# Constants first on GpSimd, and attention steps dealt out anew over the feed-forward phases

## The chip, the cores and the metric

The kernel runs on one core of one Trainium2 chip. The metric is the device time of one execution in microseconds, as the median of several runs. The core's engines are TensorE (PE, with its weight loads shown as PEld), VectorE (DVE), ScalarE (ACT), GpSimd (POOL) and SyncE (SP, used here only to issue transfers). PE matmuls write to PSUM, which has eight banks; everything else lives in SBUF or in device memory.

## The reference, cut to what matters

Everything is float32. First comes attention with a memory, for 4 batches, 8 heads, 576 positions and head width 64:

```python
scores = scale * q @ k.T                       # causal mask, softmax
local = softmax(scores) @ v
q_p = phi(q)                                   # elu(q) + 1
mem_out = (q_p @ M_prev) / (q_p @ z_prev + 1e-6)
g = sigmoid(beta)                              # one per head
attn = g * mem_out + (1 - g) * local
x = attn as 2304 tokens x 512
x = softplus(x @ w1_in) @ w1_out               # 512 -> 2048 -> 512
y = elu(x @ w2_in) @ w2_out                    # 512 -> 2048 -> 512
```

## The kernel before, in words

**Tiling of the feed-forward work.** The 2304 tokens are cut into five chunks (`CHUNKS`) of 512, 512, 448, 416 and 416 columns. A phase is one chunk through one layer, `ffn(c, layer)`. Its first half goes over 16 tiles of the inner width: each has 12 matmuls (4 slices of the contraction, three products of split values: high by high, high by low, low by high, lines 573 to 575), an activation on ACT and DVE (`act`, lines 547 to 560), and a split of the result into a high and a low part (lines 577 and 578). Its second half has 16 weight tiles with 12 matmuls each (lines 589 to 591). So there are ten phases of 384 matmuls, 32 weight tiles each, in the order that the list `order` in `TUNE` gives: chunks 0 and 1 through layer 1, the same two through layer 2, and then chunks 2, 3 and 4, both layers each.

**Weights.** They come as 64-bit numbers and are converted once each: a load on SP's queue (L504), one operation on ACT (L507) and two on DVE (L508, L509) that make a 32-bit float, a rounding copy on ACT (called through L97), a subtraction on DVE (L516), and a store of both parts to scratch memory on SP's queue (L518). Later uses load from scratch (`s_0i`, `s_0o`, `s_1i`, `s_1o`, L533). `weights` fetches a tile from scratch if it is there and converts it in place if not. The preamble converts 14 tiles of `w1_in` among its attention steps; the other weights of layer 1 are converted where phase 1 uses them. `conversions()` is a generator that converts weights of layer 2 ahead of use, into scratch, one tile per step.

**Attention** is a generator too, `attention(b, part, ...)`. Part A of a batch is its first 256 positions (21 steps), part B its last 320 (43 steps). A step issues scores on PE, the mask, scale and row minimum in one DVE instruction (L319), the exponential on ACT (L325), normalisation, transposes on PE against the identity (L360, L260), the products with v and with the memory (L375, L377, L385), and the transfers for later heads on POOL's queue (L172, L173, L180, L191 to L210). `chain` strings batches together. The preamble runs part A of batches 0 and 1; `sides()` then runs part A of batches 2 and 3 and part B of all four.

**What sets the order.** At the end of the file a loop walks the phases. Each entry of `order` holds, for either half of a phase, two shares per weight tile: how many attention steps and how many conversions are put out there. They are summed up, and a step is put out whenever the sum passes one. Attention steps are put out with a priority 400 ahead of their place, weight loads 200 ahead. The framework's planner then fixes each engine's instruction order by these priorities and by a simulation of its own; on the chip each engine works its list in that order.

**The start.** `early_loads` issues the transfers of batch 0 on SP's queue. `constants()` is called after it: the load of `beta` on POOL's queue (L110), the identity (a memset and a select on POOL, in the helper masks.py, called at L111), the mask (a memset on DVE, L112, and a select on POOL, L113), ones, and from `beta` the two gates `ig` and `iomg` on ACT and DVE (L118 to L122). A memset on POOL of a tile that only a loop of zero length (`still`) would read stands at L647, and `pads()` (L132) clears the ends of the score buffers.

Of the kernel before, what the change touches and what calls it, by code (L numbers as in the profile page):

```python
# [8 lines left out]
F32 = mybir.dt.float32  # L9
# [9 lines left out]
KD = DM // 128  # L19
# [16 lines left out]
WIDTH = [sum(n for _, _, n in c) for c in CHUNKS]  # L36
SLOT = (0, 1, 2, 0, 1)
TUNE = dict(
    st='q', pri=(200, 200), conv=(4, 2, 14), inw=4, still=0, ahead=(3, 3, 0), plain=(0, 1, 2, 3),
    hi='ssss ssss', lo='v', sc='vv vvv ssv', pt='s ssv', eva='sv',  # L40


    order=((0, 0, (1.9, 0.0), (1.1, 0.0)), (1, 0, (0.4, 0.2), (0.9, 0.9)), (0, 1, (0.9, 0.0), (0.9, 0.0)), (1, 1, (1.0, 0.0), (1.3, 0.0)), (2, 0, (0.4, 0.0), (1.2, 0.0)), (2, 1, (0.8, 0.0), (1.2, 0.0)), (3, 0, (0.4, 0.0), (1.2, 0.0)), (3, 1, (0.8, 0.0), (1.0, 0.0)), (4, 0, (0.0, 0.0), (0.0, 0.0)), (4, 1, (0.0, 0.0), (0.0, 0.0))),
)


# [12 lines left out]
def kernel(  # L59
# [14 lines left out]
    nc = tc.nc  # L74
    ve, se, ge, te = nc.vector, nc.scalar, nc.gpsimd, nc.tensor
# [9 lines left out]
    psf = ctx.enter_context(tc.tile_pool(name="psf", bufs=4, space=bass.MemoryType.PSUM))  # L85
# [4 lines left out]
    T = TUNE  # L90

    def f32(ap):
        return ap.bitcast(F32)
# [8 lines left out]
    bsb = const.tile([128, H], F32, name="bsb")  # L102
    ident = const.tile([128, 128], F32, name="ident")
    mask = const.tile([128, QP], F32, name="mask")
# [2 lines left out]
    iomg = const.tile([128, H], F32, name="iomg")  # L107

    def constants():
        nc.gpsimd.dma_start(bsb, beta)  # L110
        make_identity(nc, ident)  # L111
        ve.memset(mask, 0.0)  # L112
        ge.affine_select(  # L113
            out=mask[:, 512:640], in_=mask[:, 512:640], pattern=[[-1, 128]],
            compare_op=ALU.is_ge, fill=NEG, base=0, channel_multiplier=1,
        )
        ve.memset(ones, 1.0)
        se.activation(ig, bsb, ACTF.Exp, scale=-1.0)  # L118
        ve.tensor_scalar(ig, ig, 1.0, None, ALU.add)
        ve.reciprocal(iomg, ig)  # L120
        ve.tensor_scalar(iomg, iomg, -1.0, 1.0, ALU.mult, ALU.add)
        ve.reciprocal(iomg, iomg)  # L122

    sph = [const.tile([128, SOFF[4] + QP], F32, name=f"sph{i}") for i in range(2)]
    slots = [[const.tile([128, 2, 512], F32R, name=f"x{c}_{k}") for k in range(KD)] for c in range(2)]
# [4 lines left out]
    def pads():  # L130
        for t in sph:
            ge.memset(t[:, SOFF[4] + S:], 0.0)  # L132
# [397 lines left out]
    def make(src, key, pool=None):  # L530
        w = (pool or wp).tile([128, 2, 4, 128], F32R, name="w", tag="g" if pool else "w")
        if key in scratch:
            nc.sync.dma_start(f32(w), scratch[key])  # L533
        else:
            convert(src, key, w)
        return w
# [70 lines left out]
    def early_loads(pool):  # L607

        d = {key: [] for key in ("kq", "q", "z", "v", "m")}
        for p in range(NP):  # L610
            if p % 2 == 0:
                pair = gp.tile([128, 2, 512], F32, name="kq", tag="g")
            kq = pair[:, p % 2, :]
            t = pool.tile([128, 6, 128], F32, name=f"ar0_{p}")
            for h in range(2):
                own = slice(64 * h, 64 * h + 64)
                nc.sync.dma_start(kq[own], ak[p, own, h, :])
            nc.sync.dma_start(t, ar[p])
            d["kq"].append(kq)
            d["q"].append(t[:, 0:2, :])  # L620
            d["z"].append(t[:, 2:3, :])
            d["v"].append(t[:, 3:5, :].rearrange("p h (t c) -> p h t c", t=2))
            d["m"].append(t[:, 5, :].rearrange("p (h c) -> p h c", h=2))
        return d
# [3 lines left out]
    def chain(parts, ahead):  # L628

        parts, active = list(parts), []  # L630
        while parts or active:
            if parts and (not active or len(active) == 1 and active[0][2] <= ahead):
                b, part, pool, early = parts.pop(0)
                active.append([(b, part), attention(b, part, pool, early), 21 if part == "A" else 43])
            for a in list(active):
                a[2] -= 1
                if next(a[1], a) is a:
                    active.remove(a)
                    ready.add(a[0])
                else:  # L640
                    yield

    with tc.tile_pool(name="pre", bufs=1) as pre, tc.tile_pool(name="pre3", bufs=2) as pre3:
        loads = early_loads(pre)
        constants()
        still = slots[1][KD - 1]
        ge.memset(f32(still), 0.0)  # L647
        k = 0
        begin, step, count = T["conv"]
        for _ in chain(((0, "A", pre3, loads), (1, "A", pre3, None)), T["ahead"][0]):  # L650
            if k == 0:
                pads()
            if k >= begin and (k - begin) % step == 0 and len(made) < count:
                key = f"0i{len(made)}"
                made[key] = make(w1i[len(made)], key, gp if len(made) < count - T["inw"] else None)
            for _ in range(T["still"]):
                h = psf.tile([128, 512], F32, name="h", tag="h")
                tc.keep_in_program_order(te.matmul(h, still[:, 0, 0:128], still[:, 0, :], start=True, stop=True))
            k += 1
    late = ctx.enter_context(tc.tile_pool(name="late", bufs=1))  # L660
    slots.append([late.tile([128, 2, WIDTH[2]], F32R, name=f"x2_{k}") for k in range(KD)])
# [98 lines left out]
```

## Time and profile before

| what | value |
|---|---|
| median of 3 runs | 1108.59 us (1107.11 to 1111.91) |
| the profiled execution | 1105.83 us |
| its span, first to last instruction | 1104.1 us |
| PE busy | 1058.9 us, 96% of the span |
| PE weight loads busy | 913.4 us, 83% |
| DVE busy | 688.0 us, 62% |
| ACT busy | 672.2 us, 61% |
| POOL busy | 91.1 us, 8% |
| transfers | 252.71 MB, 229 GB/s on the mean |

The profile lists each instruction with its engine and its line in the program. Busy time is the union of the spans of an engine's instructions. The granted clock of PE is given as a share of full speed (2.4 GHz). The DMA share is the mean busy share of the core's 16 DMA engines. A name such as `w<-in_w2i` is the tile written and the tile or tensor read.

### The profile page before, as it was taken

Reading aid. Unit: us, or ns where it says so; the run is one execution under the profiler, and the core shown is the slowest. Engines: PE = TensorE matmul, PEld = TensorE weight load, DVE = VectorE, ACT = ScalarE, POOL = GpSimd, SP = SyncE. Lnnn points to the kernel's source line nnn. Section 1 sums busy time; section 2 is a strip of 40 time slices with the busy share of each in tenths; the row PEclk is TensorE's granted clock in tenths of the full one; section 3 lists DMA queues with packets and bytes.
Section 4 is the critical chain, followed back from the end, with each engine's and each line's share of the span. In section 5 each row is a group of like instructions: output and inputs, shape, how many; then the busy total and the mean of one; then the engine's idle time right before and its main releaser. Section 6 shows DMA issues by size and latency. Waiting matters only on the chain.

```text
span 1104.1 us, 15804 instructions
## 1 busy us (share of the span) xinstructions
PE 1058.9 (96%) x5328; PEld 913.4 (83%) x5328; DVE 688.0 (62%) x1698; ACT 672.2 (61%) x1458; POOL 91.1 (8%) x173
## 2 busy tenths in 40 slices
PE   4799999999899999999999999999999999999998
PEld 2356766767687888888889999999999999999998
DVE  5974686677776788688746755984576472150540
ACT  4755885478875896567747964664696452290330
POOL 6123132100000000100000000000000000000000
PEclk8778999999999999999999999999999999999999
DMA  9891278768899758955666656657755567877785
GB/s 283 302 297 50 84 242 265 244 223 279 295 314 340 256 197 303 328 192 182 197 205 222 227 176 231 218 186 234 241 174 182 172 212 237 258 235 232 227 236 179
DMA packets 73409, 252.71 MB, mean 229 GB/s; under 512 B 10352, under 2 KB 14960, under 8 KB 73328
## 3 DMA queue, kind: packets, MB, share of 16 engines
q1 hardware_dynamic: 64720, 217.61, 59.0%
q0 software_dynamic: 8608, 34.09, 10.2%
q8 instruction: 42, 0.69, 0.3%
q14 instruction: 39, 0.32, 0.1%
HBM read 213.39 MB, written 38.27 MB: 228 GB/s over the span
## 4 chain that ended last, share of the span: by engine, by line
PE 80%; DMA 9%; DVE 7%; ACT 2%; issue 1%; SPq 0%; POOL 0%; DVEq 0%; ACTq 0%
PE h L573 11%; PE h L574 11%; PE h L575 11%; PE h L589 10%; PE h L591 10%; PE h L590 10%; PE tp L360 4%; PE o L377 2%; PE o L385 2%; DMA s_1i<-w 2%; PE s L297 2%; DMA w<-in_w2i 2%; DMA w<-in_w2o 2%; PE o L375 2%; DMA w<-in_w1i 1%; PE s L293 1%
## 5 line engine op out<-in xcount | busy, mean ns | idle before, releaser
L573 PE MATMUL h<-x,w 128*128 128x512 f32 (+2 forms) x640 | 239.4, 379 | 8.4 <-DVE t L552 4.2
L589 PE MATMUL h<-g,w 128*128 128x512 f32 (+2 forms) x640 | 238.2, 374 | 2.6 <-DMA w<-s_0o 2.6
L574 PE MATMUL h<-x,w 128*128 128x512 f32 (+2 forms) x640 | 240.1, 375 | 0.0
L575 PE MATMUL h<-x,w 128*128 128x512 f32 (+2 forms) x640 | 239.2, 374 | 0.0
L591 PE MATMUL h<-g,w 128*128 128x512 f32 (+2 forms) x640 | 238.4, 373 | 0.0
L590 PE MATMUL h<-g,w 128*128 128x512 f32 (+2 forms) x640 | 238.4, 373 | 0.0
L573 PEld LDWEIGHTS h<-x,w 128*128 128x128 f32 x640 | 121.0, 190 | 25.7 <-DVE t L552 5.8
L589 PEld LDWEIGHTS h<-g,w 128*128 128x128 f32 x640 | 120.8, 189 | 15.2 <-DMA w<-s_0o 3.1
L574 PEld LDWEIGHTS h<-x,w 128*128 128x128 f32 x640 | 121.2, 189 | 13.3 <-issue 1.7
L575 PEld LDWEIGHTS h<-x,w 128*128 128x128 f32 x640 | 121.3, 190 | 12.8
L591 PEld LDWEIGHTS h<-g,w 128*128 128x128 f32 x640 | 120.7, 189 | 12.6 <-issue 1.4
L590 PEld LDWEIGHTS h<-g,w 128*128 128x128 f32 x640 | 120.9, 189 | 11.9 <-issue 0.7
L578 DVE TENSOR_TENSOR g<-t,g 128x512 fp32r<-128x512 f32 (+2 forms) x160 | 100.7, 633 | 31.3 <-ACT g L577 30.4
L325 ACT ACTIVATE sph<-sph,neg 128x576 f32<-128x576 f32 (+3 forms) x160 | 96.2, 602 | 35.4 <-DVE neg L319 34.9
L577 ACT CAST g<-t 128x512 fp32r<-128x512 f32 (+2 forms) x160 | 91.4, 574 | 31.0 <-DVE t L560 25.6
L552 DVE SCALAR_TENSOR_TENSOR t<-h,t 128x512 f32<-128x512 f32 (+2 forms) x80 | 50.4, 635 | 56.6 <-ACT t L551 56.2
L365 ACT CAST ptb<-tp 128x512 fp32r<-128x512 f32 (+2 forms) x96 | 44.2, 498 | 55.0 <-PE tp L360 54.7
L366 DVE TENSOR_TENSOR ptb<-tp,ptb 128x512 fp32r<-128x512 f32 (+2 forms) x96 | 53.0, 574 | 38.2 <-ACT ptb L365 37.6
L319 DVE CUSTOM_DVE_ANT_0 sph<-s,mask 128x128 f32<-128x128 f32 (+4 forms) x80 | 38.4, 482 | 60.1 <-PE s L297 39.9
L360 PE MATMUL tp<-ident,sph 128*128 128x128 f32 x480 | 71.1, 282 | 0.2 <-DVE sph L335 0.2
L507 ACT ACTIVATE wr<-w 128x512 f32<-128x512 f32 x64 | 42.8, 669 | 41.7 <-DMA w<-in_w2i 15.0
L360 PEld LDWEIGHTS tp<-ident,sph 128*128 128x128 f32 x480 | 59.8, 146 | 8.2 <-DVE sph L335 1.5
(112 smaller groups left out, 1539.2 us busy)
## 6 DMA issues: line engine op xcount, KB each, us to landing
w<-s_1i SPq DMA_DIRECT2D x80, 512.0 KB, 3.9
w<-s_1o SPq DMA_DIRECT2D x65, 512.0 KB, 4.2
w<-s_0i SPq DMA_DIRECT2D x64, 512.0 KB, 4.2
w<-s_0o SPq DMA_DIRECT2D x64, 512.0 KB, 4.3
qk<-in_qk POOLq DMA_DIRECT2D x32, 480.0 KB, 5.5
w<-in_w1i SPq DMA_DIRECT2D x16, 512.0 KB, 5.5
s_0i<-w SPq DMA_DIRECT2D x16, 512.0 KB, 4.4
w<-in_w1o SPq DMA_DIRECT2D x16, 512.0 KB, 4.7
```

The lines of the kernel that those rows point to most:

```text
L325: se.activation(Pi, Pi, ACTF.Exp, scale=-1.0, bias=neg[:, i:i + 1], accum_out=sums(n, i))
L360: te.transpose(pt[:, c:c + 128], P[:, poff(n, i) + 128 * j:poff(n, i) + 128 * j + 128], ident)
L366: ve.tensor_sub(dst[:, 1, :c], pt[:, :c], f32(dst)[:, 0, :c])
L552: ve.scalar_tensor_tensor(t, h, 0.0, t, ALU.max, ALU.add)
L573: te.matmul(h[:, :N], hi[:, k, :], xk[:, 0, :N], start=k == 0, stop=False)
L574: te.matmul(h[:, :N], hi[:, k, :], xk[:, 1, :N], start=False, stop=False)
L575: te.matmul(h[:, :N], lo[:, k, :], xk[:, 0, :N], start=False, stop=k == KD - 1)
L577: se.copy(g[:, 0, :N], t[:, :N])
L578: ve.tensor_sub(g[:, 1, :N], t[:, :N], f32(g)[:, 0, :N])
L589: te.matmul(h[:, :N], hi[:, k, :], gs[f][:, 0, :N], start=f == 0, stop=False)
L590: te.matmul(h[:, :N], hi[:, k, :], gs[f][:, 1, :N], start=False, stop=False)
L591: te.matmul(h[:, :N], lo[:, k, :], gs[f][:, 0, :N], start=False, stop=f == KF - 1)
```

## The change

`constants()` is called ahead of `early_loads` and with a priority of 1000. Inside it POOL now makes the part of the mask that holds the triangle by itself (memset and select), then the identity, and then issues the load of `beta`; DVE clears only the rest of the mask. The memset of L647 and the empty loop go. The place of `pads()` becomes an entry of `TUNE`, with the same value, zero. In `order` the shares of the first four phases are other numbers: fewer attention steps in the second half of phase 1 and in phase 2, more in phases 3 and 4; conversions ahead of layer 2 begin in the second half of phase 1 and are fewer in the second half of phase 2.

```diff
 TUNE = dict(
-    st='q', pri=(200, 200), conv=(4, 2, 14), inw=4, still=0, ahead=(3, 3, 0), plain=(0, 1, 2, 3),
+    st='q', pri=(200, 200), conv=(4, 2, 14), inw=4, ahead=(3, 3, 0), pads=0, plain=(0, 1, 2, 3),
...
-    order=((0, 0, (1.9, 0.0), (1.1, 0.0)), (1, 0, (0.4, 0.2), (0.9, 0.9)), (0, 1, (0.9, 0.0), (0.9, 0.0)), (1, 1, (1.0, 0.0), (1.3, 0.0)), (2, 0, ...
+    order=((0, 0, (1.9, 0.0), (0.8, 0.2)), (1, 0, (0.2, 0.2), (0.8, 0.6)), (0, 1, (1.1, 0.0), (1.2, 0.0)), (1, 1, (1.1, 0.0), (1.5, 0.0)), (2, 0, ...
 )
@@ constants()
-        nc.gpsimd.dma_start(bsb, beta)
-        make_identity(nc, ident)
-        ve.memset(mask, 0.0)
+        ge.memset(mask[:, 512:640], 0.0)
         ge.affine_select(
             out=mask[:, 512:640], in_=mask[:, 512:640], pattern=[[-1, 128]],
             compare_op=ALU.is_ge, fill=NEG, base=0, channel_multiplier=1,
         )
+        make_identity(nc, ident)
+        nc.gpsimd.dma_start(bsb, beta)
+        ve.memset(mask[:, 0:512], 0.0)
         ve.memset(ones, 1.0)
@@ the preamble
+        with tc.high_priority(offset=1000):
+            constants()
         loads = early_loads(pre)
-        constants()
-        still = slots[1][KD - 1]
-        ge.memset(f32(still), 0.0)
         k = 0
         begin, step, count = T["conv"]
         for _ in chain(((0, "A", pre3, loads), (1, "A", pre3, None)), T["ahead"][0]):
-            if k == 0:
+            if k == T["pads"]:
                 pads()
             if k >= begin and (k - begin) % step == 0 and len(made) < count:
                 key = f"0i{len(made)}"
                 made[key] = make(w1i[len(made)], key, gp if len(made) < count - T["inw"] else None)
-            for _ in range(T["still"]):
-                h = psf.tile([128, 512], F32, name="h", tag="h")
-                tc.keep_in_program_order(te.matmul(h, still[:, 0, 0:128], still[:, 0, :], start=True, stop=True))
             k += 1
```

## Rows read from the trace of the kernel before

**Rows 1.** The page: busy us, share of the span, instructions.
```profile
PE 1058.9 (96%) x5328; PEld 913.4 (83%) x5328; DVE 688.0 (62%) x1698; ACT 672.2 (61%) x1458; POOL 91.1 (8%) x173
```

**Rows 2.** Stretches: length, busy PE, PEld, DVE, ACT, POOL; clock, DMA share, GB/s.
```profile
0.00:20.00 20.00, 7.28 (x24) 5.26 (x24) 7.16 (x30) 5.53 (x15) 14.85 (x33) 1.00 0.88 252
20.00:72.00 52.00, 39.61 (x143) 21.73 (x143) 47.65 (x175) 40.34 (x119) 10.58 (x20) 0.67 0.92 314
...
155.90:226.80 70.90, 70.90 (x309) 49.19 (x309) 49.00 (x139) 40.18 (x99) 12.61 (x23) 1.00 0.73 245
226.80:296.10 69.30, 60.57 (x276) 46.70 (x275) 52.72 (x116) 58.87 (x119) 3.73 (x8) 0.98 0.79 269
296.10:355.70 59.60, 56.82 (x276) 47.56 (x275) 41.32 (x95) 36.83 (x74) 2.68 (x5) 0.97 0.92 317
355.70:411.80 56.10, 56.10 (x277) 47.14 (x276) 44.38 (x98) 47.07 (x95) 2.15 (x4) 1.00 0.67 236
411.80:466.30 54.50, 54.42 (x271) 45.73 (x270) 41.42 (x95) 35.65 (x74) 3.86 (x7) 1.00 0.91 323
466.30:524.70 58.40, 57.19 (x283) 48.05 (x283) 49.86 (x111) 39.79 (x83) 3.22 (x6) 1.00 0.55 186
524.70:585.80 61.10, 61.10 (x321) 52.30 (x320) 38.66 (x103) 34.96 (x78) 4.30 (x8) 1.00 0.65 204
585.80:636.60 50.80, 50.70 (x279) 46.68 (x278) 36.03 (x85) 46.46 (x99) 2.69 (x5) 1.00 0.66 218
```

**Rows 3.** Waits of PE before 72 us: us in total, times, longest.
```profile
PE h L293 <- DVE neg L319: 10.4, 5, 5.2
```

**Rows 4.** Timeline of the first 14 us: start, length, engine, line, tiles.
```profile
1.24 0.67 POOL L110 DMA_DIRECT2D bsb<-in_beta  x1 [0.80 <-POOLq L743]
1.91 0.22 POOL masks.py:197 MEMSET ident<- 128x128 f32 x1
2.05 0.97 POOL L647 MEMSET x<- 128x1024 f32 x1
...
3.12 0.54 POOL L172 DMA_DIRECT2D kq<-in_qk  x1
...
3.61 1.42 PE L293 MATMUL h<-kq 64*128 64x128 f32 x4 [3.61 <-DMA kq<-in_ak]
...
3.80 0.21 ACT L118 ACTIVATE ig<-bsb 128x8 f32<-128x8 f32 x1 [1.78 <-DMA bsb<-in_beta]
...
7.08 0.33 POOL L113 TENSOR_SCALAR_AFFINE_SELECT mask<-mask 128x128 f32<-128x128 f32 x1
...
8.43 0.32 POOL masks.py:199 TENSOR_SCALAR_AFFINE_SELECT ident<-ident 128x128 f32<-128x128 f32 x1
8.52 3.36 SPq L504 DMA_DIRECT2D w<-in_w1i  x3
...
14.19 0.28 DVE L319 CUSTOM_DVE_ANT_0 sph<-h,mask 128x128 f32<-128x128 f32 x1
```

**Rows 5.** Waits of PE from 200 to 360 us.
```profile
PE h L573 <- DVE t L552: 4.2, 3, 1.8
PE h L589 <- DMA w<-s_0o: 2.6, 1, 2.6
```

**Rows 6.** Chain of waits from 220 to 360 us: start, length, what.
```profile
228.37 0.47 PE h L573 x2
...
267.17 0.43 PE h L574
...
340.24 9.90 DMA w<-s_0o
```

**Rows 7.** ACT's groups of instructions in phase 2: busy, mean ns | idle before.
```profile
L507 ACT ACTIVATE wr<-w 128x512 f32<-128x512 f32 x17 | 11.4, 668 | 16.5 <-DMA w<-in_w2i 15.0 <-DMA w<-in_w2o 1.5
...
L97 ACT CAST w<-wr 128x512 fp32r<-128x512 f32 x16 | 9.9, 619 | 2.8 <-DVE wr L509 1.8 <-ACT w L97 0.8 <-ACT R L97 0.2
```

**Rows 8.** Line 297 alone in phase 4's second half: length, PE, PEld.
```profile
524.70:585.80 61.10, 7.35 (x30) 5.51 (x30) 1.00 0.65 204
```

More of the change, by code (lines that the diff above doesn't have):

```diff
@@ L38 @@
 TUNE = dict(
-    st='q', pri=(200, 200), conv=(4, 2, 14), inw=4, still=0, ahead=(3, 3, 0), plain=(0, 1, 2, 3),
+    st='q', pri=(200, 200), conv=(4, 2, 14), inw=4, ahead=(3, 3, 0), pads=0, plain=(0, 1, 2, 3),
     hi='ssss ssss', lo='v', sc='vv vvv ssv', pt='s ssv', eva='sv',
-    order=((0, 0, (1.9, 0.0), (1.1, 0.0)), (1, 0, (0.4, 0.2), (0.9, 0.9)), (0, 1, (0.9, 0.0), (0.9, 0.0)), (1, 1, (1.0, 0.0), (1.3, 0.0)), (2, 0, (0.4, 0.0), (1.2, 0.0)), (2, 1, (0.8, 0.0), (1.2, 0.0)), (3, 0, (0.4, 0.0), (1.2, 0.0)), (3, 1, (0.8, 0.0), (1.0, 0.0)), (4, 0, (0.0, 0.0), (0.0, 0.0)), (4, 1, (0.0, 0.0), (0.0, 0.0))),
+    order=((0, 0, (1.9, 0.0), (0.8, 0.2)), (1, 0, (0.2, 0.2), (0.8, 0.6)), (0, 1, (1.1, 0.0), (1.2, 0.0)), (1, 1, (1.1, 0.0), (1.5, 0.0)), (2, 0, (0.4, 0.0), (1.2, 0.0)), (2, 1, (0.8, 0.0), (1.2, 0.0)), (3, 0, (0.4, 0.0), (1.2, 0.0)), (3, 1, (0.8, 0.0), (1.0, 0.0)), (4, 0, (0.0, 0.0), (0.0, 0.0)), (4, 1, (0.0, 0.0), (0.0, 0.0))),
 )
```

## The prediction

> **What bounds the kernel now.** I read the page's busy line first: TensorE (PE) is busy 96% of the span [rows 1], so only its holes can be won and only added holes can lose. The busy times by stretch [rows 2] show where they are. The cuts are the times at which the ten feed-forward phases begin, and the middle of each of the first four. PE is idle for 12.7 of the first 20 us and 12.4 of the next 52, and in the latter its clock is granted at 0.67 on the mean. Phase 2 (226.8 to 355.7 us) has 8.7 us of idle PE in its first half and 2.8 in its second; phase 3 has 0.1, the first half of phase 4 has 1.2. After that PE is full, and nothing that the change does there can pay.
>
> The waits say who ends these holes. At the start it is the mask-and-minimum instruction of VectorE (DVE), L319: 10.4 us in five waits [rows 3]. The first scores are done at 3.6 us, but L319 first runs at 14.19 us [rows 4]. Its mask is ready at 7.41, because GpSimd's (POOL's) select stands behind seven of its load issues; by then DVE is in the feature work of the first two head pairs, the second of which waits for a load, and L319 stands behind both in DVE's order. In phase 2, PE waits for the FFN's own activation (L552) and for a weight load, `s_0o` [rows 5]; the chain of waits shows that load landing after 9.9 us [rows 6]. ScalarE (ACT) sits idle for 15.0 us in phase 2 in front of L507, the first instruction of a weight conversion, until its load has landed [rows 7]. ACT takes its work in order, so the FFN's activations stand behind that instruction, PSUM banks come free late, and PE stops. Each long hole is followed by matmuls at half rate: 0.43 us each, where two took 0.47 [rows 6]. Seven or eight such matmuls after 263 us and as many after 350 us cost 0.2 us each, so some 3 us. All of phase 2's loss is then 8.7 + 2.8 + 3 = 14.5 us.
>
> **What the steps do.** A list of share per weight tile decides how many attention steps and how many weight conversions are put out in each half phase. Summing the shares, with whole steps taken as they come due:
> - attention steps: phase 1 30+18 becomes 30+13, phase 2 6+14 becomes 3+13, phase 3 14+14 becomes 17+19, phase 4 16+20 becomes 17+24. The sum to the end of phase 4 is 132 before and 136 after; the phases behind keep their shares, and the 214 steps end in phase 7 in place of phase 8.
> - conversions ahead of layer 2: 0 in phase 1 and 17 in phase 2 become 3 and 12. The 16th tile of `w2i` and the first of `w2o` are then converted where they are used, in phase 3, which spares one reload.
>
> Price of a step, from the second half of phase 4: 61.1 us with 192 FFN matmuls at 0.235 us (45.1 us) leave 16.0 us for 30 records of L297, that is 3.75 heads at eight records. A head is 43/8 = 5.4 steps, so a step costs PE 0.8 us. DVE spent 38.66 us on them, 1.9 us a step; ACT 34.96 less four copies of 0.6, so 1.6 us a step [rows 2, 6 to 8]. A conversion costs ACT 0.67 + 0.62 = 1.29 us [rows 7] and moves 0.5 MB each way. PE's own work only changes its place: moved steps count at zero, except for holes.
>
> **Phase 2.** By its shares the first half loses three steps, and it starts five steps less far advanced; I take four fewer in that stretch, and two conversions fewer. ACT falls from 58.87 by 6.4 and 2.6 to 49.9 us; the stretch without holes is 60.57 less 3.2, so 57.4 us: ACT at 87%. The nearest row is the first half of phase 5, ACT at 46.46 of 50.8 us (91%) with 0.1 us of idle PE [rows 2]. The holes could therefore go altogether. But they were made by an in-order wait for a load, and conversions remain; bounds 0 and 8.7 us left, I take 3 and 0.5 of half rate, a gain of 8.7 + 1.5 - 3.5 = 6.7. In the second half 14 conversions by the shares become 9, some 5 MB less out of 317 GB/s x 59.6 us = 18.9 MB [rows 2], so the late `s_0o` load has room. Of 2.8 idle and 1.5 of half rate I take 3 as gained (bounds 0 and 4.3). Phase 2: -9.7 us, between 0 and -14.5.
>
> **Phase 1.** Three conversions join its second half, whose transfers were 245 x 70.9 = 17.4 MB; with 3 MB more in 4 us less it is 305 GB/s. Two rows stand near: 323 GB/s with 0.1 us of idle PE (phase 3, second half) and 317 GB/s with 2.8 (phase 2, second half) [rows 2]. ACT and DVE are at 57 and 69% there, and lose five steps. I take +0.5; bounds 0 and 4.3.
>
> **Phases 3 and 4.** DVE is the fuller engine: first half of phase 3 44.38 + 3 x 1.9 of 56.1 + 2.4, second 41.42 + 5 x 1.9 of 54.5 + 4.0, first of phase 4 49.86 + 1.9 of 58.4 + 0.8: 86, 87 and 87%. The last stood at 85% with 1.2 us of idle PE [rows 2]. I take 1 us more for each of the three, +3. Lower bound 0; upper the 8.7 us of phase 2's first half, the fullest row.
>
> **The start.** POOL now makes memset, select, memset, select before the beta load: 0.22 + 0.33 + 0.22 + 0.32 = 1.1 us from 1.24, so the mask is ready near 1.8 and the identity near 2.4 us. The memset of L647 (0.97 us) goes, so its first load issues at about 3.1 to 3.4, as before (3.12); the two selects no longer stand between the loads. Both ways this is under 0.7 us, and I cost it at nothing: the SP queue, which brings the first batch, does not stand behind POOL, and issues the first weight load at 8.52 [rows 4]. A new wait: beta now lands 1.1 us later, near 4.9 us, and the reciprocal chain behind it on ACT and DVE (0.21 us on ACT, then four small DVE operations) ends near 6. If it stands ahead of L319, the first scores wait until then, not until 4.3; still 8 us before 14.19, so it costs nothing unless it holds ACT's first exponentials (at most 2 us).
>
> L319 can then run when keys land. DVE has 7.16 us of work in its first 20 us and 47.65 in the next 52 [rows 2]; what moves forward comes out of the second stretch. Upper bound: 14.19 - 4.3 = 9.9 us, if DVE alone paced the stretch. But the transfers are nearly full: 252 x 20 + 314 x 52 = 21.4 MB by 72 us. At the 323 GB/s of the busiest row [rows 2] these take 66 us, so about 6 can be had; and the conversions wait for their loads, not for DVE alone. Lower bound: a loss of 2. I take -3.
>
> The Trainium skill, "DMA: Bandwidth & Descriptors", section "Issuing engines are not separate DMA queues", says that loads started by several engines run on the same 16 DMA engines and interleave. The trace agrees, with a DMA share of 0.92 over 52 us [rows 2]. By it alone the start gains nothing, which is the first rival.
>
> **Sum.** -9.7 + 0.5 + 3 - 3 = -9.2. The profiled execution took 1105.83 us around a span of 1104.1; it would become 1096.6. The median of the three runs, 1108.59, lies 2.8 above it: 1099.4, and I say 1099.
>
> **Rivals.**
> 1. The start is paced by transfers and gains nothing; the rest as above: 1108.6 - 6.2 = 1102. For it: the DMA share. Against it: 0.88 in the first 20 us, at 252 GB/s, is not full. Chance 0.15.
> 2. The head start carries through whole, with 6 us, and phase 2's holes close but for 2: -6 - 12.5 + 2 = -16.5, 1092. For it: the 10.4 us behind L319, and phase 5's row. Against it: loads pace the conversions. Chance 0.13.
> 3. The pressure only changes place: phase 2 keeps half its loss (-7), phases 3 and 4 get 4 us of holes, phase 1 1.5: -1.5, 1107. For it: DVE at 86 to 87% in three stretches. Against it: ACT at 91% in phase 5 leaves PE whole. Chance 0.18. That the new shares change nothing because the planner draws steps forward anyway gives the same time and is counted here.
> 4. Slower: the second half of phase 3. It holds all 16 inline conversions of `w2o` (at 323 GB/s) and now five more steps with their loads. If DVE, which has to end each conversion before PE can use the tile, falls behind there, every weight tile comes late, and PE gets holes and half rate as at 350 us: 2.8 + 1.5 us per such case. Three there and two in the first half of phase 4 are +21; with a gain of 12 elsewhere +9, 1118. It decides from the point where DVE's work exceeds some 95% of the stretch; I reckon 87%. Chance 0.14.
>
> The forecast itself has 0.40, its own range 1094 to 1104. Two runs of this kernel can be told apart at about 0.5%, 5.5 us: faster means under 1103, slower over 1114. Faster: 0.37 of the forecast's, two thirds of rival 1, all of rival 2: 0.60. Slower: rival 4 and 0.01: 0.15. The rest, 0.25, is no change. The range that leaves out 2 in 10: 1086 to 1112.
>
> **What would show it.** L319 first before 6 us, and the wait for it at the start under 4 us; the first FFN matmul (72.0 us) at 66 to 71; phase 2's idle PE under 6 us in all and no half-rate stretch at its end; ACT's wait for `w2i` under 11 us; idle PE in phases 3 and 4 between 2 and 6 us; attention gone before phase 8. The prediction is wrong if phase 2 keeps its holes, or if phases 3 and 4 get more than 8 us of them.

## The result and the profile after

The changed kernel took 1096.03 us (median of four runs, 1086.98 to 1096.56) beside 1110.25 for the kernel before on the same chip (1107.11 to 1113.39). The ratio is 0.9872, with a 95% interval of 0.9829 to 0.9915. Run again later, unaltered, it took 1093.37 us, ratio 0.9852 (0.9813 to 0.9892). So the forecast of 1099 was 3 us too high, inside the range, and "faster", which the prediction sets at under 1103, was right. The profiled execution took 1096.56 us around a span of 1094.8.

In the code after, lines from about 110 on carry numbers one higher: L319 is now L320, L552 is L553, L573 is L574. The busy line of the page after, to set beside [rows 1]:

```profile
PE 1063.1 (97%) x5328; PEld 914.8 (84%) x5328; DVE 685.1 (63%) x1698; ACT 672.4 (61%) x1458; POOL 91.0 (8%) x173
```

PE has as many instructions as before and is busy for 4.2 us longer in a span that is 9.3 us shorter. The next view says where. Stretches of the kernel after, with the columns of [rows 2]; the cuts are again the first matmul of each phase and the middle of phases 1 to 4:

```profile
0.00:20.00 20.00, 12.33 (x37) 7.33 (x38) 10.92 (x58) 10.61 (x35) 14.16 (x33) 1.00 0.90 251
20.00:72.50 52.50, 45.13 (x138) 24.70 (x138) 38.88 (x140) 33.09 (x93) 10.26 (x19) 1.00 0.76 256
72.50:152.20 79.70, 77.07 (x343) 51.43 (x341) 50.31 (x146) 60.78 (x139) 20.66 (x37) 1.00 0.51 168
152.20:217.40 65.20, 65.20 (x282) 45.56 (x282) 50.97 (x143) 40.08 (x94) 13.49 (x25) 1.00 0.89 302
217.40:282.20 64.80, 57.92 (x244) 44.09 (x243) 40.97 (x87) 50.44 (x97) 3.42 (x7) 0.95 0.79 275
282.20:338.80 56.60, 55.16 (x272) 45.72 (x271) 33.96 (x80) 30.90 (x65) 3.28 (x6) 1.00 0.81 278
338.80:398.90 60.10, 60.10 (x308) 50.99 (x308) 51.13 (x115) 53.74 (x110) 1.20 (x2) 1.00 0.66 224
398.90:456.00 57.10, 56.95 (x290) 48.51 (x289) 50.88 (x124) 43.49 (x91) 6.14 (x11) 1.00 0.88 303
456.00:516.20 60.20, 59.81 (x307) 50.46 (x306) 53.52 (x119) 43.45 (x93) 3.23 (x6) 1.00 0.64 209
516.20:575.90 59.70, 59.70 (x309) 51.11 (x308) 37.84 (x104) 32.82 (x75) 4.91 (x9) 1.00 0.65 206
```

PE's idle time is the length less the first number. Phase 2 had 8.7 and 2.8 us of it and now has 6.9 and 1.4. Phases 3 and 4 had 1.3 up to 524.7 us and now have 0.6 up to 516.2. The start had 12.7 and 12.4 and now has 7.7 and 7.4, 10.1 less, and yet the first feed-forward matmul comes at 72.53 us where it came at 72.0. PE was busy for 57.5 us there in place of 46.9: the idle time won at the start was filled by matmuls that took longer.

The first instructions moved as worked out. Timeline of the kernel after, one line for each of mask, identity, the end of the `beta` chain on ACT, the first mask-and-minimum, and the first feed-forward matmuls:

```profile
2.05 0.30 POOL L111 TENSOR_SCALAR_AFFINE_SELECT mask<-mask 128x128 f32<-128x128 f32 x1
2.38 0.30 POOL masks.py:199 TENSOR_SCALAR_AFFINE_SELECT ident<-ident 128x128 f32<-128x128 f32 x1
...
3.91 0.21 ACT L119 ACTIVATE ig<-bsb 128x8 f32<-128x8 f32 x1 [1.90 <-DMA bsb<-in_beta]
...
4.68 0.29 DVE L320 CUSTOM_DVE_ANT_0 sph<-h,mask 128x128 f32<-128x128 f32 x1 [3.27 <-PE h L294]
...
72.53 1.18 PE L574 MATMUL h<-x,w 128*128 128x512 f32 x4
```

The mask is ready at 2.35 us in place of 7.41, and the first mask-and-minimum runs at 4.68 in place of 14.19 [rows 4]. It waits only for the scores; the later `beta` hinders nobody. Waits of PE before 72.5 us, after:

```profile
PE h L294 <- DMA kq<-in_ak: 7.7, 5, 3.7
...
PE h L294 <- DVE neg L320: 0.3, 1, 0.3
```

The 10.4 us of [rows 3] are 0.3. The largest wait left at the start is that for the keys' own loads. Waits of PE from 200 to 345 us, after, against [rows 5]:

```profile
PE h L574 <- DMA w<-s_0i: 5.2, 1, 5.2
PE h L590 <- DMA w<-s_0o: 1.2, 1, 1.2
PE h L298 <- DVE t L553: 1.2, 1, 1.2
```

The wait for the activation, 4.2 us in three, is gone from phase 2's feed-forward matmuls. The main hole is now another one, a weight load.

### The profile page after: what moved, and what is told of

It reads as the page before. It is cut to its first block, busy times and chain, and to the rows that moved or that the text cites. A ratio compares the mean times of both kernels' runs of the same rounds, so it can differ in the third digit from the quotient of the medians.

```text
span 1094.8 us, 15781 instructions
## 1 busy us (share of the span) xinstructions
PE 1063.1 (97%) x5328; PEld 914.8 (84%) x5328; DVE 685.1 (63%) x1698; ACT 672.4 (61%) x1458; POOL 91.0 (8%) x173
## 3 DMA queue, kind: packets, MB, share of 16 engines
q0 software_dynamic: 8608, 34.09, 10.4%
## 4 chain that ended last, share of the span: by engine, by line
PE 86%; DMA 6%; DVE 4%; ACT 2%; issue 1%; SPq 0%; ACTq 0%; DVEq 0%
PE h L590 11%; PE h L574 11%; PE h L592 11%; PE h L591 11%; PE h L575 11%; PE h L576 11%; PE tp L361 5%; PE o L378 3%; PE o L386 2%; PE s L298 2%; DMA w<-in_w2i 2%; PE o L376 2%; PE s L294 1%; PE h L298 1%; PE o L387 1%; DMA w<-in_w1i 1%
## 5 line engine op out<-in xcount | busy, mean ns | idle before, releaser
L574 PE MATMUL h<-x,w 128*128 128x512 f32 (+2 forms) x640 | 238.3, 378 | 9.4 <-DMA w<-s_0i 5.2
L574 PEld LDWEIGHTS h<-x,w 128*128 128x128 f32 x640 | 120.7, 189 | 25.2 <-DVE g L579 5.6
L326 ACT ACTIVATE sph<-sph,neg 128x576 f32<-128x576 f32 (+2 forms) x160 | 96.4, 603 | 43.5 <-DVE neg L320 43.0
L553 DVE SCALAR_TENSOR_TENSOR t<-h,t 128x512 f32<-128x512 f32 (+2 forms) x80 | 50.7, 637 | 62.3 <-ACT t L552 62.0
L366 ACT CAST ptb<-tp 128x512 fp32r<-128x512 f32 (+2 forms) x96 | 44.9, 498 | 47.3 <-PE tp L361 46.9
L320 DVE CUSTOM_DVE_ANT_0 sph<-s,mask 128x128 f32<-128x128 f32 (+4 forms) x80 | 38.5, 483 | 54.4 <-PE s L298 37.4
L361 PE MATMUL tp<-ident,sph 128*128 128x128 f32 x480 | 71.1, 282 | 0.4 <-DVE sph L336 0.4
L361 PEld LDWEIGHTS tp<-ident,sph 128*128 128x128 f32 x480 | 59.9, 146 | 7.3 <-DVE sph L336 1.0
L560 ACT ACTIVATE t<-t 128x416 f32<-128x416 f32 (+2 forms) x64 | 36.8, 579 | 40.6 <-DVE t L559 37.3
```

The costliest lines, as they stand in the source:

```text
L326: se.activation(Pi, Pi, ACTF.Exp, scale=-1.0, bias=neg[:, i:i + 1], accum_out=sums(n, i))
L361: te.transpose(pt[:, c:c + 128], P[:, poff(n, i) + 128 * j:poff(n, i) + 128 * j + 128], ident)
L553: ve.scalar_tensor_tensor(t, h, 0.0, t, ALU.max, ALU.add)
L574: te.matmul(h[:, :N], hi[:, k, :], xk[:, 0, :N], start=k == 0, stop=False)
```

## Experiments

Each ratio is to the kernel before, run beside it on the same chip, with a 95% interval. "Start" is the time to the first feed-forward matmul.

### One half of the change at a time

`e1_const` is the changed kernel with the old shares; `e2_shares` is the kernel before with all the new shares; `a1_again` is the changed kernel, unaltered.

```diff
 e1_const, against the kernel after
-    order=((0, 0, (1.9, 0.0), (0.8, 0.2)), (1, 0, (0.2, 0.2), (0.8, 0.6)), (0, 1, (1.1, 0.0), (1.2, 0.0)), (1, 1, (1.1, 0.0), (1.5, 0.0)), ...
+    order=((0, 0, (1.9, 0.0), (1.1, 0.0)), (1, 0, (0.4, 0.2), (0.9, 0.9)), (0, 1, (0.9, 0.0), (0.9, 0.0)), (1, 1, (1.0, 0.0), (1.3, 0.0)), ...
 e2_shares, against the kernel before: the same line the other way round
```

> The constants part alone (constants first, no memset of the spare tile), with the shares of before. Theory A, that both parts pay: the first 156 us shrink by about 4 us as in the changed kernel and phase 2 keeps its holes (some 11 us of idle PE), so 1110 - 4 = 1106 us. Rival B, that the start gives nothing because its matmuls then run at half rate until about 71 us: 1110 us, with the first feed-forward matmul at 72 us or later and the half rate in every matmul before it.

> The new shares alone, with the constants where they were before. Theory A, that both parts pay: phase 2's idle PE falls from 11.5 to about 8 us and its length by some 7 us, phases 3 and 4 take back 2 to 4 us; the start stays at 72 us with its mixture of full and half rate: 1110 - 7 = 1103 us. Rival B, that the shares are the whole gain: 1096 us. Rival C, that they are worth nothing without the other start: 1110 us.

> The changed kernel once more, unaltered, to see how far its start varies from one execution to the next. One of its four times was 1087 us, three were 1096. If the moment at which PE's clock first rises varies, some executions come near 1087 and the profiled one shows a first rise either near 71 us again (span about 1095) or well before it (span 1085 to 1090). If the start is paced by transfers and not by the clock, all times lie at 1096 within 0.3%.

Measured: `e1_const` 1099.43 us, 0.9919 (0.9890 to 0.9948); `e2_shares` 1099.44, 0.9925 (0.9889 to 0.9960); `a1_again` 1093.37, 0.9852 (0.9813 to 0.9892); the kernel before 1108.09. Each half is worth some 8.7 us alone and both together 14.7, so they nearly add. The start is therefore worth about as much as the shares, where I had it at half of them. `e1_const` came in below both of its forecasts, 1106 and 1110, and `e2_shares` between its theory A and its rival B. The repeat's six times run from 1088.28 to 1095.12, further apart than the 0.3% of a start paced by transfers. The profiled execution of `e1_const` shows only part of the 8.7 us: it reaches the end of phase 1's first half at 151.9 us, 4.0 us before the kernel before does. Phase 2's first half with the old shares behind the new start, `e1_const`:

```profile
222.90:297.20 74.30, 63.79 (x276) 49.49 (x274) 53.66 (x116) 59.50 (x120) 3.74 (x8) 0.91 0.74 257
```

It has 10.5 us of idle PE. The new start alone does nothing for phase 2; that is the shares' doing.

### The shares, one kind at a time

`e3_att` is the kernel before with the new attention shares alone, `e4_conv` with the new conversion shares alone.

```diff
 e3_att, against the kernel before
+    order=((0, 0, (1.9, 0.0), (0.8, 0.0)), (1, 0, (0.2, 0.2), (0.8, 0.9)), (0, 1, (1.1, 0.0), (1.2, 0.0)), (1, 1, (1.1, 0.0), (1.5, 0.0)), ...
 e4_conv, against the kernel before
+    order=((0, 0, (1.9, 0.0), (1.1, 0.2)), (1, 0, (0.4, 0.2), (0.9, 0.6)), (0, 1, (0.9, 0.0), (0.9, 0.0)), (1, 1, (1.0, 0.0), (1.3, 0.0)), ...
```

> The kernel before with the new attention shares alone; conversions ahead stay at 3 and 14 in phase 2. Theory A, that phase 2 loses its holes because the conversions' loads are fewer there: nearly all of phase 2's idle PE stays (9 to 11 us), total 1106 to 1110 us. Rival B, that ACT and DVE have too much attention there: idle PE in phase 2 falls to 7 to 8 us as with all new shares, total 1100 us.

> The kernel before with the new conversion shares alone (3 in phase 1's second half, 12 in phase 2); attention stays as before. Theory A, that the conversions' loads make phase 2's holes: idle PE there falls to 4 to 8 us, no late load at its end, total 1099 to 1103 us. Rival B, that it is the attention: idle PE stays at 9 to 11 us, total 1107 to 1110 us.

Measured: `e3_att` 1103.0 us, 0.9977 (0.9954 to 1.0001); `e4_conv` 1106.54, 1.0009 (0.9981 to 1.0036); before 1106.65. Neither alone is told from no change, `e3_att` only just. Waits of PE in phase 2's first half in `e3_att`, which has 11.1 us of idle PE there (70.6 less 59.52):

```profile
PE h L573 <- DVE t L552: 5.5, 1, 5.5
PE h L573 <- DMA w<-s_0i: 3.5, 1, 3.5
```

These are theory A's holes, at a time below its 1106 to 1110. Fewer attention steps alone leave the activation late. The second half of phase 1 and the first of phase 2 in `e4_conv`, columns as in [rows 2]:

```profile
156.90:232.50 75.60, 73.34 (x312) 50.26 (x312) 55.21 (x155) 45.17 (x109) 13.15 (x24) 0.98 0.74 252
232.50:302.00 69.50, 61.58 (x273) 48.51 (x272) 49.21 (x107) 57.07 (x113) 3.72 (x8) 0.93 0.80 288
```

Three conversions put there without thinning the attention make phase 1's second half 4.7 us longer than [rows 2] has it, with 2.3 us of idle PE. In phase 2 they do what theory A said: idle PE falls from 11.5 to 7.9 us, all of it in the first half, and the two halves take 123.1 us in place of 128.9. One nearly cancels the other. After the change, with five steps fewer, the same three make no hole (65.20 of 65.20 us busy). From the end of phase 1's first half to the end of the kernel, the profiled executions took 948.2 us before, 948.9 in `e1_const`, 948.5 in `e3_att`, 947.8 in `e4_conv`, and 942.6, 942.0 and 941.7 in the kernel after, its repeat and `e2_shares`. The shares are worth 6 us there, and only both kinds together.

### The mask alone

`m1_latemask` is the changed kernel with only the mask made as before, behind the loads; identity and `beta` stay ahead.

```diff
 constants()
-        ge.memset(mask[:, 512:640], 0.0)
-        ge.affine_select(out=mask[:, 512:640], ...)
...
-        ve.memset(mask[:, 0:512], 0.0)
...
         loads = early_loads(pre)
+        ve.memset(mask, 0.0)
+        ge.affine_select(out=mask[:, 512:640], ...)
```

> The changed kernel with the mask alone made as before: cleared whole on DVE and selected on POOL behind the load issues; identity, beta and the missing memset stay as changed. Theory A, that the mask's place in front of the first scores is what the constants part is worth: L319's counterpart first runs at 12 to 15 us again, PE's wait for it in the preamble is back at 8 to 12 us, and the time is that of the new shares alone, 1099 us. Rival B, that the missing memset or the identity is the cause: 1093 us, like the changed kernel.

Measured: 1099.89 us, 0.9954 (0.9932 to 0.9976). `q1_pool` below, the same program with the mask early and one queue changed, took 1093.7 on that chip, 0.9907 (0.9875 to 0.9940). By the times, as theory A has it, without the early mask only about the shares' own worth is left. Timeline, waits of PE and the whole start as one stretch, `m1_latemask`, where the mask-and-minimum is L314:

```profile
16.68 0.28 DVE L314 CUSTOM_DVE_ANT_0 sph<-h,mask 128x128 f32<-128x128 f32 x1
```

```profile
PE h L288 <- DVE neg L314: 4.2, 3, 2.5
```

```profile
0.00:74.00 74.00, 60.09 (x174) 32.92 (x175) 56.31 (x211) 46.66 (x134) 24.39 (x51) 1.00 0.86 282
```

It is 2.5 us later than before, and PE waits for it again, though for 4.2 us and not the 8 to 12 that theory A forecast. PE's idle time in this start is 13.9 us, no more than the 15.0 of the kernel after, where the mask is early. All of the loss in this execution stands in PE's busy time, 60.1 us, of which the next section tells. That the early mask is worth some 6 us rests on the times; by which path is not shown.

### What sets the length of the start

In four kernels of this study PE works the same instructions at the start in the same order as in the one after, as their first 500 PE rows show: its repeat, `q1_pool`, `s2_more1b` and `n2_noconv2`; `e1_const` differs only from the second half of phase 1. Three run the order of before. Reading the start of every profiled execution as one stretch gives this table (us):

```
order   kernel        start   PE busy   PE idle   wait for mask-and-minimum
before  before        72.0    46.9      25.1      10.4
before  e2_shares     71.2    47.3      23.9       9.2
before  e3_att        72.3    47.2      25.1      10.1
before  e4_conv       72.6    50.2      22.4       9.8
after   s2_more1b     61.5    44.7      16.8      under 1.8
after   n2_noconv2    64.6    47.7      16.9      under 1.8
after   q1_pool       68.4    54.2      14.2       1.5
after   a1_again      69.5    54.4      15.1      under 2.2
after   e1_const      70.7    56.3      14.4      under 1.7
after   after         72.5    57.5      15.0       0.3
```

Where no length is given, the wait is not among the four longest. The stretches of the kernel before, the one after and `s2_more1b`:

```profile
0.00:72.00 72.00, 46.89 (x167) 26.99 (x167) 54.81 (x205) 45.86 (x133) 25.43 (x52) 0.76 0.91 297
```

```profile
0.00:72.50 72.50, 57.46 (x174) 32.03 (x175) 49.80 (x197) 43.70 (x127) 24.42 (x52) 1.00 0.80 255
```

```profile
0.00:61.50 61.50, 44.73 (x175) 25.80 (x175) 48.19 (x194) 42.90 (x128) 24.55 (x52) 0.92 0.89 286
```

The new order takes 8.7 us of idle PE away on the mean (24.1 to 15.4), and at least 5.5 between any two executions. What it gives back is in PE's busy time, 44.7 to 57.5 us for the same work. Among its six executions the idle time hardly moves, 14.2 to 16.9 us, and the start goes with the busy time. Line L378 (L377 before) up to the first feed-forward matmul, same three kernels in the same order; the columns are count, busy us, mean ns of one, idle before:

```profile
L377 PE MATMUL o<-pt,ar 128*64 128x256 f32 (+1 forms) x40 | 11.9, 435 | 3.6 <-ACT pt L97 3.6
```

```profile
L378 PE MATMUL o<-pt,ar 128*64 128x256 f32 (+1 forms) x40 | 15.4, 540 | 1.7 <-ACT pt L97 1.7
```

```profile
L378 PE MATMUL o<-pt,ar 128*64 128x256 f32 (+1 forms) x40 | 11.0, 410 | 2.9 <-ACT pt L97 2.9
```

The same forty matmuls take 15.4 us in one execution and 11.0 in another. The timeline shows the two rates for one shape, four matmuls of L378 at 58 us, after and `s2_more1b`:

```profile
58.10 1.54 PE L378 MATMUL o<-pt,ar 128*64 128x256 f32 x4
```

```profile
58.44 0.86 PE L378 MATMUL o<-pt,ar 128*64 128x256 f32 x4
```

1.54 to 0.86 us is the step between TensorE's two levels, 1.2 and 2.4 GHz. By the granted clock and the first short matmuls, the rise came at 71.6 us in the kernel after, at 36.3 in its repeat, at 51.5 in `n2_noconv2` and at 29.0 in `s2_more1b`, with a fall in between in two of these. At about equal PE time the order is worth 6.6 to 7.7 us: `n2_noconv2` starts at 64.6 us with 47.7 of busy PE, and the kernel before, `e2_shares` and `e3_att` at 71.2 to 72.3 with 46.9 to 47.3.

Two kernels tried to turn the clock up by extra work whose results nobody reads. `w2_after` puts two matmuls of 512 columns on a zero tile ahead of each of the 42 steps at the start, held in program order. `wb2` puts two on a tile of ones ahead of the scores of each of the first 16 heads, into the bank that the scores then overwrite.

```diff
 w2_after, against the kernel after
+        ve.memset(f32(still), 0.0)
...
+            for _ in range(2):
+                h = psf.tile([128, 512], F32, name="h", tag="h")
+                tc.keep_in_program_order(te.matmul(h, still[:, 0, 0:128], still[:, 0, :], start=True, stop=True))
 wb2, against the kernel after
+        ve.memset(f32(still)[:, 0, :], 1.0)
...
-                        ps = ps if i else bank(n)
+                        if not i:
+                            ps = bank(n)
+                            if b < 2:
+                                for _ in range(2):
+                                    te.matmul(ps, still[:, 0, 0:128], still[:, 0, :], start=True, stop=True)
```

> The changed kernel with two additional matmuls of 512 columns on a zeroed tile in each of the preamble's 42 attention steps; their result is never read. They cost 84 x 0.43 = 36 us of PE at half rate or 18 us at full rate. Theory A, that PE at half rate paces the start (57 us of its 72 are spent in half-rate matmuls): the clock rises before 20 us, the 57 us shrink to some 29 and with the extra 18 still fit: first feed-forward matmul at 62 to 67 us, total 1087 to 1091 us. Rival B, that transfers and conversions pace the start: 1096 us with the clock high. Rival C, that the clock does not rise or that the extra work costs more than it gives: 1100 us or more.

> The changed kernel with two additional matmuls of 512 columns (on a tile of ones, into the bank that the head's scores then overwrite, never read) ahead of the scores of each of the 16 heads of the preamble: 32 x 0.43 = 14 us of PE at half rate, 7 at full, and no ban on feed-forward work beside them, unlike the earlier run with 84. Theory A, that PE at half rate paces the start: the clock rises before 20 us and stays, the first feed-forward matmul comes at 62 to 66 us, total 1086 to 1090 us. Rival B, that the start is paced by conversions and their transfers: the first feed-forward matmul stays near 70 us whatever the clock, total 1093 to 1097 us. Rival C, that the clock does not rise earlier: 1098 us or more.

Measured: `w2_after` 1108.11 us, 0.9995 (0.9971 to 1.0019); `wb2` 1101.8, 0.9951 (0.9921 to 0.9981). Both are slower than the changed kernel, at the times of rival C in either forecast. The first tells little: the extra matmuls, bound to program order, kept the feed-forward work out until 99.4 us. The second is cleaner. Its clock rose at 6.9 us and fell at 10.3. The stretch from 10 to 50 us in `wb2`:

```profile
10.00:50.00 40.00, 38.78 (x98) 20.59 (x97) 25.21 (x104) 22.84 (x76) 12.08 (x21) 0.50 0.71 239
```

PE is busy for 38.8 of 40 us at a granted clock of 0.50, and the start takes 80.1 us, 7.6 more than in the kernel after. 2.0 us of that are PE's wait for the clearing of the additional tile. Work added to PE at half rate lengthens the start, which fits a stretch bound by PE. Extra work did not hold the clock up.

### The hole that stays in phase 2

The wait for `s_0i`, 5.2 us, could be the queue's order (its load behind others on SP) or the buffers. `q1_pool` issues the loads of the conversions ahead on POOL's queue in place of SP's.

```diff
-            nc.sync.dma_start(w64.rearrange("p k n t -> p (k n t)"), src.bitcast(I32))
+            (ge if w is None else nc.sync).dma_start(w64.rearrange("p k n t -> p (k n t)"), src.bitcast(I32))
```

> The changed kernel with the loads of the conversions ahead issued on POOL's queue and not on SP's. In the changed kernel one such load held SP's queue for 8.8 us while it waited for a buffer, and the weight load behind it came so late that PE stood for 5.2 us. Theory A, that this order in the queue makes the rest of phase 2's holes: PE's wait for that load is gone, idle PE in phase 2 is 2 to 4 us where it was 8, total 1086 to 1090 us. Rival B, that the transfers themselves are too slow there, or that POOL's own loads of keys and values now come late: 1093 us or more.

Measured: 1093.7 us, 0.9907 (0.9875 to 0.9940), and the wait as long as before. Waits of PE in phase 2 and of the SP queue from 205 to 245 us, `q1_pool`:

```profile
PE h L574 <- DMA w<-s_0i: 5.2, 1, 5.2
```

```profile
SPq L519 <- DVE w L517: 16.5, 3, 12.4
```

SP then stands up to 12.4 us in front of a store of a converted tile, and PE's wait is the same 5.2 us. The time is rival B's, 1093 or more. The loads of `s_0i` leave as they did, 2.3 us after the last slice of the phase's input is written (231.45 and 233.70 us, against the 234.09 and 236.35 below). The queue's order was not the cause. The timeline of the kernel after shows what comes before these loads:

```profile
234.09 0.37 ACT L142 CAST x<-o 128x256 fp32r<-128x256 f32 x1 [0.23 <-PE o L378]
...
236.35 2.34 SPq L534 DMA_DIRECT2D w<-s_0i  x4
```

and so does its chain of waits:

```profile
236.35 6.47 DMA w<-s_0i
242.95 0.77 PE h L574
```

The last slice of phase 2's input is attention output, written at 234.09 us, 16.7 us into the phase. Until then the first four weight tiles can't be finished and hold all four weight buffers, and all four PSUM tiles of the feed-forward matmuls (`psf`) too. The weight buffers come free together, the next loads are issued at 236.35, and the first lands 6.47 us later. The load is not the only thing that PE needs there. In the repeat, where the slice comes 16.7 us into the phase too, the same hole ends with the activation of these tiles on DVE, `a1_again`:

```profile
240.79 0.48 PE L574 MATMUL h<-x,w 128*128 128x512 f32 x1 [4.58 <-DVE g L579]
```

In the kernel after, the same instruction on DVE (it began at 241.48 us and took some 0.64) ended only 0.7 us before the load landed, so a faster load alone would have won little. What both have in common is the late slice. Of the ten executions in the table above, those in which it came 16.7 us or more into phase 2 (the kernel after, `a1_again`, `q1_pool`, `n2_noconv2`, `e2_shares`, `e3_att`) had a hole of 3.0 to 5.2 us behind it, which ended with the load of `s_0i`, in `a1_again` with the activation. In the other four it came at 12.0 us or earlier, and PE never waited for `s_0i` in that half.

With that slice earlier the wait should go; `s2_more1b` has more attention in the half phase before. `n2_noconv2` asks the other question, what the conversions cost in phase 2, and has none there.

```diff
 s2_more1b: (0, 0, (1.9, 0.0), (0.8, 0.2)) becomes (0, 0, (1.9, 0.0), (1.0, 0.2))
 n2_noconv2: (1, 0, (0.2, 0.2), (0.8, 0.6)) becomes (1, 0, (0.2, 0.0), (0.8, 0.0))
```

> The changed kernel with 1.0 in place of 0.8 attention steps per weight tile in the second half of phase 1 (16 steps and not 13). In the changed kernel the last slice of phase 2's input is written at 234 us, 17 us into that phase: its first four tiles wait for it with all four weight buffers, which then come free at once, and the next weight load lands after PE has stood for 5.2 us. Theory A, that this is the rest of phase 2's holes: the last slice comes 3 to 6 us into the phase, the 5.2 us and some 2.4 us of half rate behind them go, total 1085 to 1088 us. Rival B, that the holes follow from ACT's and DVE's load and come elsewhere: idle PE in phase 2 stays at 6 to 8 us, total 1092 to 1096 us.

> The changed kernel with no conversions ahead in phase 2 at all: three in phase 1's second half, the other 13 tiles of w2_in converted where phase 3 uses them. Theory A, that phase 2's first half keeps some 7 us of idle PE because ACT, which works in order, stands in front of conversions whose loads have not landed: without conversions its idle PE falls to 0 to 3 us, while phase 3's first half, with 13 x 1.29 us more on an ACT that had 54 of 60 us, gets 5 to 10 us of holes; total 1092 to 1100 us. Rival B, that attention and activations alone make the holes there: 5 to 8 us of idle PE stay in phase 2's first half, total 1100 us or more.

Measured: `s2_more1b` 1091.43 us, 0.9870 (0.9821 to 0.9919), before 1108.13; `n2_noconv2` 1093.04, 0.9880 (0.9823 to 0.9938), before 1108.52. By their ratios neither is told apart from the changed kernel. Waits of PE from 216 to 336 us, `s2_more1b`:

```profile
PE h L574 <- DVE neg L320: 4.5, 1, 4.5
PE h L574 <- DVE t L553: 3.1, 2, 2.8
```

The slice came at 225.96 us, 9.7 us into the phase, where the forecast had 3 to 6. The wait for `s_0i` is gone, as the buffers' account has it, and two others stand in its place: DVE, late with the mask-and-minimum and with the activation. Idle PE in that half is 7.8 us, where it was 6.9: about rival B's holes, at a time just under B's. The first halves of phases 2 and 3 in `n2_noconv2`:

```profile
210.20:270.50 60.30, 55.57 (x244) 41.83 (x243) 30.42 (x68) 43.72 (x84) 2.66 (x6) 1.00 0.52 177
...
324.70:396.30 71.60, 63.43 (x309) 50.91 (x307) 66.63 (x148) 64.48 (x134) 2.40 (x5) 1.00 0.75 256
```

Without conversions ahead, phase 2's first half keeps 4.7 us of idle PE, more than theory A's 0 to 3 and less than rival B's 5 to 8, and the largest of its waits of PE is again the one behind the late slice:

```profile
PE h L574 <- DMA w<-s_0i: 3.0, 1, 3.0
```

Phase 2 becomes 6.9 us shorter in both halves together (114.5 us in place of 121.4), and phase 3's first half 11.5 longer, with 8.2 us of idle PE at 93% DVE and 90% ACT. From the end of phase 1's first half it comes out 5.3 us behind the kernel after (947.9 to 942.6). In the profiled execution a start of 64.6 us makes up for it.

## Why the prediction was right, point by point

**The sum was right and its two large terms were not.** In the profiled pair the time to the end of phase 1's first half fell by 3.7 us (155.9 to 152.2) and the rest by 5.6 (948.2 to 942.6). I had written -3 and -6.2. The medians lie further apart, 14.2 us: the profiled execution of before, at 1105.83, was shorter than any of the four timed beside the change, and that of after the longest of its four. That -9.2 met the pair's -9.3 is luck: PE's idle time fell by 13.5 us and its busy time rose by 4.2, and the sum has no term for busy time at the start. Of the -3.7, nothing stands in the start itself (72.0 to 72.5 us). It stands in phase 1's first half, 83.9 to 79.7 us, where PE's busy time fell from 81.24 to 77.07: 45 transposes of L361 and L261 are left there where there were 50, the others being done in the start, and less of it runs at half rate.

**Phase 2: right in direction, mis-sized.** Of -9.7, idle PE gave 3.2: 11.5 became 8.3. The two half phases together are 7.5 us shorter than before (128.9 to 121.4), and part of that is attention that moved on. The work in the first half was forecast well: 49.9 us of ACT and 57.4 of PE against 50.44 and 57.92. The step that failed is "I take 3 and 0.5 of half rate" for the first half: 6.9 us of holes were left. I looked only at what had made the old holes, ACT standing in front of a conversion's load. That wait did shrink; ACT in phase 2, after, against the 15.0 us of [rows 7]:

```profile
ACT wr L508 <- DMA w<-in_w2i: 13.2, 5, 4.9
```

It came five times in place of ten, but I had said under 11 us. What I put at nothing is the tie of the first four tiles to the last slice of attention. [rows 5] could not show it, since there the slice came 12.0 us into the phase; the kernel before:

```profile
238.83 0.37 ACT L141 CAST x<-o 128x256 fp32r<-128x256 f32 x1
```

The change takes five steps out just ahead of the phase, the slice comes 16.7 us into it, and the hole behind it is 5.2 us. `e3_att` shows this wait and the old one for the activation in one phase, 3.5 and 5.5 us. I should have asked when the phase's last input is written. The second half is as forecast but for size (2.8 became 1.4).

**Phase 1: right.** I took +0.5 for three conversions in its second half; the trace has no hole there at 302 GB/s. That they fit only because attention left is `e4_conv`'s reading, 2.3 us of holes without it.

**Phases 3 and 4: wrong, to the good.** I had +3 for DVE at 86 to 87%. DVE came to 85, 89 and 89% (51.13 of 60.1, 50.88 of 57.1, 53.52 of 60.2), and idle PE is 0.0, 0.15 and 0.4 us. A DVE at 89% made no holes here; that what PE needs next stood ahead in DVE's order would explain it, but was not tested. At 93%, in `n2_noconv2`, there were 8.2 us of them, with ACT at 90% beside it. PE's waits there are for masks, activations and attention on DVE and ACT, none for a converted weight tile, so rival 4's mechanism is not shown by them. The row that I called the fullest for the upper bound, phase 2's first half, was so by neither engine: DVE 76% there and 85% in phase 4, ACT 85% there and 91% in phase 5. Rival 3, pressure that only changes place, is what `s2_more1b` and `n2_noconv2` do, not the change. The attention steps ended before phase 8, as said.

**The start: right, but the bound named was wrong.** I took -3 because "the transfers are nearly full". The DMA share of the stretch fell from 0.92 to 0.76 [rows 2] while the start stayed at 72 us, so transfers didn't pace it after the change, and rival 1's reason falls. Nor did the 21.4 MB have to arrive, on which my 66 us rest: by the table's stretches the first feed-forward matmul came after 255 x 72.5 = 18.5 MB in the kernel after, and after 286 x 61.5 = 17.6 MB in `s2_more1b`, at 61.5 us. The Trainium skill, "DMA: Bandwidth & Descriptors", section "Issuing engines are not separate DMA queues", has loads of several engines share the same DMA engines; no run here speaks against that, but here it limits nothing. Rival 2, the head start carried through whole, was priced at 6 us; PE's idle time fell by 10.1, near the upper bound of 9.9, and the length followed only where the clock rose early: 61.5 us in `s2_more1b`, 72.5 in the profiled execution. (The first scores begin at 3.6 us [rows 4]; I had written that they are done by then.) I had read a mean clock of 0.67 in [rows 2] and given it no price. Half rate was the larger term: 46.9 us of busy PE before, 44.7 to 57.5 after.

**What would show it.** L319 before 6 us and a wait under 4 us at the start: yes (4.68 and 0.3). First feed-forward matmul at 66 to 71 us: no in that execution, yes in the repeat and `q1_pool` (69.5, 68.4). Phase 2's idle PE under 6 us: no, 8.3. ACT's wait under 11: no, 13.2. Idle PE of 2 to 6 us in phases 3 and 4: no, less than 1. Three misses in one sum partly cancelled, so the forecast is better than its working.

**Open.** Why the clock rises at 29 us in one execution and at 71.6 in another with the same instructions was not settled. The order of before shows less spread (46.9 to 50.2 us of busy PE in four); whether its longer idle stretches have a part in that was not tried.

## What to carry to other kernels

When an instruction everybody waits for is moved to the front, ask what the engine behind it does with the time: here PE used it, but at half rate, and by execution the start was between 0.5 us longer and 10.5 us shorter. When you take away the wait that ends last, look for the next one by following when each input of that stretch is written and each buffer comes free, and ask whether the change moves it: the list of waits of the old kernel can't show it. Thinning one kind of filler work and moving another can pay only together: neither of the two changes of shares could be told from nothing alone.

## What the runs showed of the hardware that was not expected

The same PE instructions at the start kept PE busy between 44.7 and 57.5 us, by how much of them ran at half rate, a difference of 12.8 us. The runs of the kernel after spread over 9.6 us (1086.98 to 1096.56); that this is the same thing is likely but not shown, since only profiled executions show their start.

The granted clock can't be read as it stands ahead of its first change in the trace. It shows 1.00 for the first 72.5 us of the kernel after, in which the four matmuls of L378 took 1.54 us, and 0.92 for the start of `s2_more1b`, where four such matmuls take 1.54 us at 25 us and 0.86 at 58. Compare the duration of one shape with its duration elsewhere.

A PE that is busy for 38.8 of 40 us can stay at 0.50 all that time (`wb2`), with the small attention matmuls of this start and 22 recorded wide ones among them.
